# Queries of batch 1: transposed by DMA instead of TensorE, with a new order of all engines and loads

## The chip, the core and the metric

The kernel runs on one core of one Trainium2 chip. The metric is the device time of an execution in microseconds, as the median over runs. One more execution is recorded by the hardware profiler; its page, with all times from the first instruction on, is what is read here.

## The reference

Block-sorted attention for 4 batches of 8 heads (768 positions, 64 wide, 8 blocks of 96), then a Fourier mixing layer and an MLP on the 4 x 768 x 512 result.

```python
P = sort_net                                  # B, H, 8, 8; five Sinkhorn rounds
...
k_sorted = einsum('bhij,bhjcd->bhicd', P, k_blocks)
v_sorted = einsum('bhij,bhjcd->bhicd', P, v_blocks)
scores = scale * matmul(q_block, k_sorted_block^T)
attn = softmax(scores)
x = matmul(attn, v_sorted_block)              # then heads side by side: B, S, 512
mixed = real(fft(fft(x, axis=1), axis=2))
u = x + mixed
un = (u - mean) / sqrt(var + 1e-6)
out = u + maximum(un @ w_ch1, 0) @ w_ch2      # 512 -> 2048 -> 512
```

## The kernel before

The program is a list of operations, each with the engines that can do it, a cost, the tiles that it reads and writes and a priority. A planner (class Plan) runs through a model of the five engines in Python when the kernel is built, gives each operation an engine and a place, and the instructions are then written out in that fixed order. On the chip each engine follows its own list and waits only for semaphores. NUDGE is a table of corrections to the priorities; a smaller priority goes first. An operation on the way to the first MLP is marked as critical and gets a priority of -1000 less the time that still lies behind it; loads are excepted from that.

Of a load the planner knows the bytes. All loads share one modelled stream of Plan.HBM = 390 GB/s (counted in the f32 bytes that are read) and land 2.2 us after it. A DMA transpose, in contrast, is SP time of 1.4 us with a latency of 6.0 us, and carries no bytes:

```python
P.add({"SP": (1.4, 6.0)}, lambda _: nc.sync.dma_start_transpose(...), ..., tag="qX")
```

Loads from HBM are issued by POOL (the helper at L707), and cast f32 to f16 on the way. v of batches 0 and 1 and of batches 2 and 3 come as two tensors of two halves each; k and q come by batch and half (four heads); w1sb in four quarters, w2sb in four quarters. The large loads are all started within the first 40 us or so.

For each batch, attn does four head pairs. kqt (from L1150 on) mixes the blocks of k on TensorE (L1168), evicts it to a tile ks, and makes q's transpose qt. For batches 0 and 1 that is twelve TensorE transposes per pair of heads (L1199), tag qT, and one copy of 128 x 768 out of PSUM by ACT or DVE (L908, tag qtev). For batches 2 and 3, named in QB, load_qk fetches q by single heads, each partition getting a run of 64 elements from each of six places, and one dma_start_transpose on SP's queue (L1186) writes qt. scores (L1227) multiplies, ACT takes the exponent (L1236), L1251 or L1249 subtract one, and av (L1266) multiplies with the mixed v.

Then follow, per batch, the Fourier stages dft1 (L1340 to L1350) and dft2 (L1419, L1431, L1435), which reads the tile rb. The rows of rb are filled by four small copies by SP (a_rows, L1147). After the normalisation, batch 0 is transposed by TensorE (L1528), batches 1 to 3 by DMA (L1520), and the MLP begins: ff1 (L1549) reads w1sb, the second layer (L1606) w2sb. Batches 2 and 3 use a scheme with seven products instead of eight (L1685, L1785).

k and q of batch 1 do not lie in the tile kq but in parts of hr[1], a buffer of the MLP that is still free then (slots 8 to 11).

Of the kernel before, what the change touches and what calls it, by code (L numbers as in the profile page):

```python
# [35 lines left out]
    ('arow', -40.0, 0): 2.49, ('atd', 14.0): -43.53, ('atd', 14.0, 1): 216.41,  # L36
    ('atd', 14.0, 3): -279.13, ('atp', -40.0, 1): 7.79,
# [3 lines left out]
    ('bdk', -90.0, 0): -3.64, ('bdk', -60.0): -1.48, ('bdk', -60.0, 0): 5.16,  # L41
# [3 lines left out]
    ('bna', 20.5): -162.22, ('bna', 40.0): -493.32, ('dft1', 55.0): -1408.65,  # L45
# [8 lines left out]
    ('exp', -80.0, 0): 0.99, ('exp', -80.0, 2): 0.94,  # L54
    ('exp', -80.0, 11): 1.17, ('exp', 10.0): -1038.47,
    ('exp', 10.0, 0): 316.12, ('exp', 10.0, 1): 250.78,
    ('exp', 10.0, 10): -26.46, ('exp', 10.0, 12): 149.24,
    ('exp', 30.0, 0): -340.47, ('exp', 30.0, 4): 130.12,
    ('exp', 30.0, 8): 11.8, ('exp', 30.0, 11): 384.99,
    ('exp', 50.0): -1497.06, ('exp', 50.0, 9): 139.28,  # L60
    ('exp', 50.0, 12): 417.05, ('exp', 50.0, 15): -7.62,
    ('fadd', -300.0): -6.77, ('fadd', -300.0, 4): 378.93,
    ('fadd', -300.0, 10): 1031.06, ('fadd', -300.0, 18): -27.7,
    ('fadd', -300.0, 39): -74.85, ('fadd', -300.0, 40): -359.8,
# [63 lines left out]
    ('ksev', -80.0, 2): -2.56, ('ksev', 10.0): -153.67,  # L128
    ('ksev', 30.0, 4): -239.73, ('ksev', 30.0, 6): -81.13,
    ('ksev', 30.0, 7): -224.44, ('ln', -29.0): -227.5,  # L130
    ('ln', 20.0, 2): -195.03, ('lt', -29.5): -1.65, ('lt', 20.5): 837.52,
    ('lt', 55.5, 1): 117.13, ('mbdk', 50.0): 960.77,
    ('mbdk', 50.0, 0): 242.27, ('norm', -80.0): -10.2,
    ('norm', 10.0, 1): 14.84, ('norm', 10.0, 3): 23.14, ('norm', 30.0): -14.8,
    ('norm', 30.0, 4): 740.67, ('norm', 50.0, 3): -167.68,
    ('oo', 20.0, 0): -370.96, ('pc', -301.0, 16): -181.95,
    ('pk', -70.0, 1): 1.89, ('pmc', -30.0, 0): -4.19, ('pmc', 55.0): -63.31,
    ('pmt', 20.4): 1160.32, ('pmt', 40.0, 0): -47.38, ('pmt', 40.0, 1): -7.96,
    ('pmt', 40.4, 0): -304.8, ('pmt', 55.0, 0): -11.08,
    ('pmt', 55.0, 1): -9.84, ('pmt', 55.0, 2): 529.66,  # L140
    ('pmt', 55.0, 3): 67.16, ('pmt', 55.4, 0): -7.4, ('psa', -40.0): 1.4,
    ('psm', -75.0, 2): 1.23, ('psr', -40.0, 0): 3.56, ('psx', -40.0): 4.36,
    ('qT', 10.0): 67.2, ('qT', 10.0, 0): 32.15, ('qT', 10.0, 1): -345.76,
    ('qT', 10.0, 2): 175.76, ('qtev', -80.0, 0): -0.21,
    ('qtev', 10.0, 3): 148.76, ('relu', -300.0): -61.87,
    ('relu', -300.0, 77): 74.06, ('relu', -300.0, 83): 190.34,
    ('relu', -300.0, 117): 300.59, ('relu', -300.0, 119): 729.75,
    ('relu', -300.0, 125): 206.25, ('res', -300.0): -25.11,
    ('res', -300.0, 11): 93.78, ('res', -300.0, 26): -219.21,
    ('res', -300.0, 28): 40.94, ('res', -300.0, 33): -6.82,  # L150
# [25 lines left out]
QB = (2, 3)  # L176
# [407 lines left out]
def kernel(  # L584
# [84 lines left out]
    rv = ct("rv", [64, DM], F16)  # L669
# [1334 lines left out]
```

## Time and profile before

| | us |
|---|---|
| median of 3 runs | 259.36 (259.25 to 259.37) |
| profiled execution, its time | 258.93 |
| profiled execution, its span | 257.2 |
| PE busy | 247.5 (96%) |
| DVE busy | 240.9 (94%) |
| ACT busy | 159.5 (62%) |
| POOL busy | 54.0 (21%) |

The span goes from the first to the last instruction; what lies around it makes up the difference to the execution's own time. Matmuls are pipelined and their ends are modelled, so that neighbouring groups of PE overlap in a list of instructions; the distance from start to start is the time that a group holds the engine. Of 26.45 MB that the DMA engines wrote, 18.31 MB went through POOL's queue, and almost all of that in the first 70 us.

### The profile page before, as it was taken

Reading aid. Unit: us, or ns where it says so; the run is one execution under the profiler, and the core shown is the slowest. Engines: PE = TensorE matmul, PEld = TensorE weight load, DVE = VectorE, ACT = ScalarE, POOL = GpSimd, SP = SyncE. Lnnn points to the kernel's source line nnn. Section 1 sums busy time; section 2 is a strip of 40 time slices with the busy share of each in tenths; the row PEclk is TensorE's granted clock in tenths of the full one; section 3 lists DMA queues with packets and bytes.
Section 4 is the critical chain, followed back from the end, with each engine's and each line's share of the span. In section 5 each row is a group of like instructions: output and inputs, shape, how many; then the busy total and the mean of one; then the engine's idle time right before and its main releaser. Section 6 shows DMA issues by size and latency. Waiting matters only on the chain.

```text
span 257.2 us, 6684 instructions
## 1 busy us (share of the span) xinstructions
PE 247.5 (96%) x2612; PEld 167.7 (65%) x2612; DVE 240.9 (94%) x608; ACT 159.5 (62%) x360; POOL 54.0 (21%) x81
## 2 busy tenths in 40 slices
PE   4899998999999999999999999999999999999993
PEld 1346875566755576644666657888656888567882
DVE  4799999999999999996999999999999999889993
ACT  2599897899775969918778489100988202685010
POOL 8965222324000390003100000030100011100041
PEclk9999999999999999999999999999999999999999
DMA  7999999999950499533103031221202312200015
GB/s 131 203 219 304 211 217 216 208 210 184 151 41 3 86 179 172 64 62 113 43 18 65 10 66 24 53 101 54 82 3 43 80 71 95 84 1 0 3 69 177
DMA packets 42678, 26.45 MB, mean 103 GB/s; under 512 B 30122, under 2 KB 39096, under 8 KB 42644
## 3 DMA queue, kind: packets, MB, share of 16 engines
q0 software_dynamic: 23536, 18.31, 41.9%
q1 hardware_dynamic: 19110, 7.71, 15.0%
q8 instruction: 20, 0.33, 0.5%
q14 instruction: 12, 0.10, 0.1%
HBM read 29.03 MB, written 6.29 MB: 137 GB/s over the span
## 4 chain that ended last, share of the span: by engine, by line
PE 87%; DVE 8%; DMA 3%; issue 1%; ACT 0%; DVEq 0%; POOLq 0%
PE bank L1785 21%; PE bank L1549 17%; PE bank L1685 14%; PE bank L1606 9%; PE bank L1266 4%; DMA hr<-in_v_dram 3%; PE bank L1431 3%; PE bank L1227 2%; PE bank L1340 2%; PE bank L1168 2%; PE bank L998 2%; PE bank L926 2%; DVE rt L1283 1%; PE bank L1435 1%; PE bank L1971 1%; DVE pmt L1300 1%
## 5 line engine op out<-in xcount | busy, mean ns | idle before, releaser
L1549 PE MATMUL bank<-ut,w1sb 128*128 128x384 f16 x256 | 47.1, 326 | 0.0
L1549 PEld LDWEIGHTS <-w1sb 128*128 128x128 f16 x256 | 23.3, 98 | 14.4
L1584 POOL DMA_INDIRECT out_dram<-u,rows x9 | 9.9, 1105 | 108.3 <-DVE u L1802 74.7
L1785 PEld LDWEIGHTS <-hr 128*128 128x128 f16 x288 | 28.2, 98 | 4.3
L1236 ACT ACTIVATE ex<-bank 96x384 f32<-96x384 f32 x64 | 27.9, 489 | 2.3 <-PE bank L1227 2.0
L1705 ACT COPY vsf<-bank 128x384 f32<-128x384 f32 x48 | 21.6, 484 | 11.0 <-PE bank L1685 10.4
L1561 ACT ACTIVATE hr<-bank 128x384 f16<-128x384 f32 x48 | 23.4, 492 | 8.0 <-PE bank L1549 7.7
L1693 DVE TENSOR_TENSOR hr<-bank,vsf 128x384 f16<-128x384 f32 x48 | 25.1, 553 | 1.4 <-PE bank L1685 0.7
L1816 ACT COPY ex<-bank 128x256 f32<-128x256 f32 x9 | 3.4, 373 | 36.4 <-PE bank L1785 36.3
L1606 PE MATMUL bank<-w2sb,hr 128*128 128x512 f16 x96 | 23.8, 380 | 0.0
L1785 PEld LDWEIGHTS <-vcx 128*128 128x128 f16 x216 | 21.1, 98 | 2.7
L1685 PE MATMUL bank<-ut,w1sb 128*128 128x384 f16 x96 | 20.7, 326 | 0.0
L1785 PE MATMUL bank<-w2sb,hr 128*128 128x256 f16 x144 | 18.5, 272 | 0.0
L1785 PE MATMUL bank<-kq,vcx 128*128 128x256 f16 x144 | 17.8, 273 | 0.0
L1685 PEld LDWEIGHTS <-w1sb 128*128 128x128 f16 x128 | 12.5, 98 | 7.7
L707 POOL DMA_DIRECT2D kq<-in_q_dram x18 | 14.9, 845 | 12.5 <-DMA w2sb<-in_moe_w_ch_dram 3.3
L1283 DVE TENSOR_TENSOR rt<-bank,rz 128x384 f16<-128x384 f32 x32 | 16.9, 545 | 0.1
L1251 ACT ACTIVATE eb<-ex,negone 96x384 f16<-96x384 f32 x28 | 16.8, 620 | 0.2
L1266 PEld LDWEIGHTS <-eb 97*128 97x128 f16 x416 | 15.2, 98 | 2.2 <-issue 0.3
L1266 PE MATMUL bank<-vsf,eb 97*128 97x65 f16 x416 | 16.4, 193 | 0.0
L1249 DVE TENSOR_SCALAR eb<-ex 96x384 f16<-96x384 f32 x36 | 12.5, 366 | 2.3 <-ACT ex L1236 2.3
L908 ACT CAST vsf<-bank 96x512 f16<-96x512 f32 x22 | 13.4, 683 | 1.9 <-PE bank L998 1.9
(190 smaller groups left out, 548.8 us busy)
## 6 DMA issues: line engine op xcount, KB each, us to landing
kq<-in_k_dram POOLq DMA_DIRECT2D x6, 384.0 KB, 7.9
w1sb<-in_moe_w_ch_dram POOLq DMA_DIRECT2D x4, 512.0 KB, 20.2
w2sb<-in_moe_w_ch_dram POOLq DMA_DIRECT2D x4, 512.0 KB, 21.8
hr<-in_v_dram POOLq DMA_DIRECT2D x2, 768.0 KB, 9.1
kq<-in_v_dram POOLq DMA_DIRECT2D x2, 768.0 KB, 16.2
kq<-in_q_dram POOLq DMA_DIRECT2D x16, 96.0 KB, 7.8
out_dram<-u SPq DMA_DIRECT2D x5, 256.0 KB, 2.1
kq<-in_q_dram POOLq DMA_DIRECT2D x2, 384.0 KB, 13.1
```

What stands on the lines that cost most here:

```text
L707: o = P.add({eng: c}, lambda _: e.dma_start(dst, src), r=r, w=w, prio=prio, nbytes=nbytes, tag="load", after=after)
L1236: nc.scalar.activation(ex.ap[0:96], pss[h2].ap[0:96, 0:384], AF.Exp, scale=SCALE),
L1251: nc.scalar.activation(ed, src, AF.Identity, bias=negone[0:96])
L1266: nc.tensor.matmul(po.ap[:, 65 * T:65 * T + 65], eb.ap[:, e0:e0 + 128], vsf[0:97, vi:vi + 65], start=(n == 0), stop=(n == len(WIN[T]) - 1) ...
L1283: P.add({"DVE": (0.465, 0.56)}, lambda _: V.tensor_tensor(rt.ap[:, :, D * h:D * h + D], po3()[:, :, 0:D], rz.ap[:, :, None].broadcast_to([ ...
L1549: nc.tensor.matmul(ps.ap[:, 0:GT], w1sb[:, c, 128 * fc:128 * fc + 128], ut.ap[:, c, :], start=(c == 0), stop=(c == 3))
L1561: nc.scalar.activation(hr[g][:, fc, :], ps.ap[:, 0:GT], AF.Relu)
L1606: nc.tensor.matmul(ps.ap, hr[g][:, fc, 128 * tt:128 * tt + 128], w2sb[:, fc, :], start=(fc == 0), stop=(fc == 15))
L1685: nc.tensor.matmul(ps.ap[:, 0:GT], lhs[:, c, fi], rhs()[:, c, :], start=(start and c == 0), stop=(c == 1), skip_group_check=True)
L1693: return P.add({"DVE": (0.47, 0.57)}, lambda _: V.tensor_tensor(hr[g][:, fc, :], p.ap[:, 0:GT], o.ap, op=ALU.add), r=r, w=hk(g, fc, fc + 1 ...
L1705: P.add({"ACT": act(GT)}, lambda _: nc.scalar.copy(x.ap, A.ap[:, 0:GT]), r=[A], w=[x], prio=pr_v - 1, tag="pc", after=avs)
L1785: nc.tensor.matmul(ps.ap[:, o:o + 256], lhs()[:, fc], rhs[:, fc], start=(start and fc == 0), stop=(fc == 7), skip_group_check=True)
```

## The change

The constant QB takes batch 1 in. With that, q of batch 1 is loaded by single heads (eight loads of 96 KB in place of two of 384 KB), its four pairs are transposed by DMA from SP's queue, and the 48 TensorE transposes and four copies out of PSUM are no longer there. A function slab gives the place of a slot in kq or in hr[1], which the DMA transpose and the load now need. The table NUDGE is a new one: none of its entries has the value that it had, and loads are in it for the first time.

```diff
 NUDGE = {
-    ('arow', -40.0, 0): 2.49, ('atd', 14.0): -43.53, ('atd', 14.0, 1): 216.41,
...
+    ('atd', 14.0): -258.81, ('atd', 14.0, 2): -106.46,
...
+    ('ff1', 100.0): -564.84,
...
+    ('load', -996.0, 0): -3084.429, ('load', -995.0, 0): -2492.353,
+    ('load', -993.0, 0): 1023.837, ('load', 30.0, 0): -3409.518,
+    ('load', 30.5, 0): -3302.183, ('load', 30.52, 0): -3814.411,
+    ('load', 31.0, 0): -0.289, ('load', 31.51, 0): 1.041,
+    ('load', 41.0, 0): -10.289, ('load', 62.0, 0): -31.289,
...
 }
-QB = (2, 3)
+QB = (1, 2, 3)
...
     def qk16(nm, b, hf):
-        n = slot[nm, b, hf]
-        s_ = (kq[:, n, :] if n < 8 else hr[1].rearrange("p a b -> p (a b)")[
-            :, 1536 * (n - 8):1536 * (n - 7)])
-        return s_.rearrange(
+        return slab(slot[nm, b, hf]).rearrange(
             "p (h r d) -> p h r d", h=4, r=6)
+
+    def slab(n):
+        return kq[:, n, :] if n < 8 else hr[1].rearrange(
+            "p a b -> p (a b)")[:, 1536 * (n - 8):1536 * (n - 7)]
...
         if nm == "q" and b in QB:
             for h in range(4):
-                load(kq[:, slot[nm, b, hf], :].rearrange(
+                load(slab(slot[nm, b, hf]).rearrange(
                     "p (a r h d) -> p a h r d", a=2, h=2, d=D)[
                     :, h // 2, h % 2],
                     src[b, 4 * hf + h].rearrange("(r p) d -> p r d", r=6),
-                    260000, [("kq", slot[nm, b, hf], h)], prio + 0.01 * h,
+                    260000, kqk(slot[nm, b, hf], h, h + 1), prio + 0.01 * h,
                     after=after)
...
             P.add({"SP": (1.4, 6.0)}, lambda _: nc.sync.dma_start_transpose(
                 qt.ap.rearrange("p (r s) -> p r s", r=6),
-                kq[:, slot["q", b, hf], 768 * hl:768 * hl + 768]),
+                slab(slot["q", b, hf])[:, 768 * hl:768 * hl + 768]),
                 r=kqk(slot["q", b, hf], 2 * hl, 2 * hl + 2), w=[qt],
                 tag="qX")
```

A key of NUDGE is a tag with the priority as written in the code and, as a third part, the number of the operation among those of that tag and priority. Without nudge, the loads have -994 and -993 for dtab and lt, 19 and 20 for cs and tab, 30 to 31.53 for k and q of batch 1, 31.6 and 31.8 for v of batches 2 and 3, 40 to 43 for w1sb and 62 on for w2sb and what follows.

More of the change, by code (lines that the diff above doesn't have):

```diff
@@ L35 @@
 NUDGE = {
-    ('arow', -40.0, 0): 2.49, ('atd', 14.0): -43.53, ('atd', 14.0, 1): 216.41,
-    ('atd', 14.0, 3): -279.13, ('atp', -40.0, 1): 7.79,
[3 rows of a table removed]
-    ('bdk', -90.0, 0): -3.64, ('bdk', -60.0): -1.48, ('bdk', -60.0, 0): 5.16,
[3 rows of a table removed]
-    ('bna', 20.5): -162.22, ('bna', 40.0): -493.32, ('dft1', 55.0): -1408.65,
[8 rows of a table removed]
[L54 to L64, printed above, removed]
[63 rows of a table removed]
-    ('ksev', -80.0, 2): -2.56, ('ksev', 10.0): -153.67,
-    ('ksev', 30.0, 4): -239.73, ('ksev', 30.0, 6): -81.13,
@@ L130 @@
[L130 to L150, printed above, removed]
[10 rows of a table removed]
-    ('vcd', 70.0): 509.62, ('vcd', 70.0, 2): -49.12, ('vcd', 70.0, 3): -26.03,
-    ('vcd', 70.0, 7): 344.21, ('vcp', -75.0, 1): 2.91,
-    ('vcp', -75.0, 3): 3.09, ('vcp', -75.0, 7): 10.46, ('vev', -50.0): 0.6,
@@ L164 @@
-    ('vev', -50.0, 5): 0.91, ('vev', -50.0, 7): 0.93, ('vev', 9.0, 5): 7.64,
-    ('vev', 12.0, 6): -90.32, ('vev', 12.0, 12): -11.78,
-    ('vev', 12.0, 15): -68.85, ('vmean', -55.0, 2): -1.47,
-    ('vmix', -50.0): -2.39, ('vmix', -50.0, 0): 0.84,
-    ('vmix', -50.0, 7): -7.23, ('vmix', 9.0, 5): 39.01,
-    ('vmix', 12.0): -1403.54, ('vmix', 12.0, 3): -19.6,
-    ('vmix', 12.0, 4): 74.1, ('vmix', 12.0, 5): -23.55,
-    ('vmix', 12.0, 7): -236.78, ('vmix', 12.0, 13): -29.22,
-    ('ws', 90.0, 1): 182.05, ('ws', 90.0, 2): 285.89, ('y', 40.0, 2): -109.37,
+    ('atd', 14.0): -258.81, ('atd', 14.0, 2): -106.46,
@@ new lines @@
+    ('atp', -40.0, 1): 10.64, ('atp', 14.0): 192.74, ('av', -80.0, 3): -0.69,
+    ('av', 10.0): -1020.96, ('av', 10.0, 1): 145.43, ('av', 30.0): -703.12,
+    ('av', 30.0, 3): 1022.43, ('av', 50.0): -271.95, ('bdk', -90.0): 2.31,
+    ('bdk', -60.0): 2.32, ('bdv', -60.0, 0): 1.06, ('bn', 20.0): -257.31,
+    ('bn', 40.0, 2): -198.53, ('bn', 40.5): 87.88, ('bn', 40.5, 0): 211.14,
+    ('bn', 40.5, 2): -175.08, ('bna', 20.0): -208.52, ('dft1', 40.0): -257.71,
+    ('dft1', 40.0, 1): 805.24, ('dft1', 55.0): -410.85,
@@ new lines @@
+    ('dft2', -30.0, 1): 6.25, ('dft2', -29.0, 2): -371.61,
+    ('dft2', 20.0, 2): 88.48, ('dft2', 20.5): 222.15,
+    ('dft2', 20.5, 1): -2.92, ('dft2', 20.5, 2): -2.37,
+    ('dft2', 40.5): -444.69, ('dft2', 55.0, 0): -78.1,
+    ('dft2', 55.0, 1): -23.72, ('dft2', 55.5): -201.24,
+    ('dft2', 55.5, 1): 350.58, ('dft2', 55.5, 2): 513.62,
+    ('em1', 10.0): 249.9, ('em1', 10.0, 15): -281.94, ('em1', 30.0): 325.88,
+    ('em1', 30.0, 14): -19.21, ('exp', -80.0): -4, ('exp', -80.0, 3): -1.32,
@@ new lines @@
+    ('exp', -80.0, 4): -1.72, ('exp', -80.0, 5): -5.33,
+    ('exp', -80.0, 11): -0.74, ('exp', 10.0): -524.78,
+    ('exp', 10.0, 10): 297.83, ('exp', 10.0, 12): -11.68,
+    ('exp', 10.0, 13): -17.87, ('exp', 30.0): 14.21, ('exp', 30.0, 7): 312.64,
+    ('exp', 30.0, 12): -408.4, ('exp', 30.0, 13): -37.31,
+    ('exp', 50.0, 9): 803.77, ('exp', 50.0, 14): 23.79,
+    ('exp', 50.0, 15): 262.41, ('fadd', -300.0): 121.94,
+    ('fadd', -300.0, 13): 179.2, ('fadd', -300.0, 14): -22.27,
[66 rows of a table added]
+    ('kq', 50.0, 2): -39.64, ('ksev', -80.0): 12.78, ('ksev', -80.0, 0): 3.11,
@@ new lines @@
+    ('ksev', 10.0): 98.18, ('ksev', 10.0, 1): -153.31,
+    ('ksev', 10.0, 4): -329.02, ('ksev', 10.0, 7): -266.01,
+    ('ln', -29.0, 2): 253.32, ('ln', 40.0): 42.11,
+    ('load', -996.0, 0): -3084.429, ('load', -995.0, 0): -2492.353,
[3 more added lines that the diff above has]
+    ('load', 41.0, 0): -10.289, ('load', 62.0, 0): -31.289,
+    ('load', 62.0, 1): -25.027, ('load', 62.5, 0): -31.789,
@@ new lines @@
+    ('load', 62.51, 0): -31.799, ('load', 62.52, 0): -31.683,
+    ('load', 62.53, 0): -29.952, ('load', 63.52, 0): -31.063,
+    ('load', 63.53, 0): -30.952, ('load', 64.0, 1): -33.163,
+    ('load', 64.5, 0): -33.663, ('load', 64.52, 0): -33.683,
+    ('load', 64.53, 0): -27.409, ('load', 65.52, 0): -29.431,
+    ('load', 65.53, 0): -34.691, ('lt', -29.5, 0): -1.55, ('lt', 20.0): 229.5,
+    ('lt', 20.0, 0): 170.22, ('mbdk', 30.0, 0): 234.38,
+    ('norm', -80.0, 0): -1.11, ('norm', 10.0, 2): 150.59,
@@ new lines @@
+    ('norm', 30.0, 4): 150.99, ('oo', 20.0, 0): 330.31,
+    ('pmt', -30.0, 0): 1.08, ('pmt', -29.6): 0.88, ('pmt', 20.0, 3): 1.12,
+    ('pmt', 40.0): 374.8, ('pmt', 40.0, 0): -378.76, ('pmt', 55.0, 2): 306.58,
+    ('pmt', 55.4, 0): -368.8, ('psr', 14.0, 0): -312, ('psx', 14.0): -87.92,
+    ('qT', -80.0): 4.2, ('relu', -300.0, 13): 441.92,
+    ('relu', -300.0, 64): 815.83, ('relu', -300.0, 91): 106.88,
+    ('relu', -300.0, 97): 288.27, ('res', -300.0): -574.79,
+    ('res', -300.0, 16): -16.14, ('res', -300.0, 31): 272.2,
[16 rows of a table added]
@@ new lines @@
+    ('vcd', 70.0, 0): -1605.11, ('vcd', 70.0, 2): -14.3,
+    ('vcd', 70.0, 3): -46.89, ('vcd', 70.0, 7): 520.99, ('vcp', -75.0): 7.61,
+    ('vcp', -75.0, 3): 0.42, ('vcp', -75.0, 4): -1.3,
+    ('vcp', -75.0, 6): -1.63, ('vcp', -75.0, 7): 10.14, ('vev', -50.0): 8.11,
+    ('vev', 9.0, 6): 853.35, ('vev', 12.0, 0): 42.91, ('vmean', -55.0): 6.25,
+    ('vmix', -50.0, 1): 0.61, ('vmix', -50.0, 2): 0.65,
+    ('vmix', -50.0, 3): 5.66, ('vmix', -50.0, 4): 3.78,
+    ('vmix', -50.0, 5): 0.76, ('vmix', -50.0, 6): 2.22,
@@ L173 @@
+    ('vmix', 9.0, 2): 1178, ('vmix', 9.0, 5): 300.92,
+    ('vmix', 9.0, 7): 2065.05, ('vmix', 12.0): -833.82,
+    ('vmix', 12.0, 1): -348.45, ('vmix', 12.0, 3): 11.85,
+    ('vmix', 12.0, 7): -654.64, ('vmix', 12.0, 8): -18.63,
+    ('vmix', 12.0, 15): -0.52, ('ws', 90.0): -149.02, ('ws', 90.0, 0): 3.05,
+    ('ws', 90.0, 5): 1348.25, ('y', 20.0, 0): 399.46, ('yz', -29.0): 302.55,
+    ('yz', -29.0, 0): 370.71,
 }
```

169 rows, old and new, of the table NUDGE are left out of this document.

## The prediction

> **What bounds the kernel now.** I read the stages first: busy time of each engine before the first data, up to the first MLP matmul, in the long remainder, and at the end.
>
> ```profile
> 0.00:9.00 9.00, 4.51 (x13) 1.78 (x14) 4.86 (x24) 2.30 (x5) 7.93 (x14) 1.00 0.80 153
> 9.00:51.40 42.40, 41.26 (x614) 26.28 (x613) 40.89 (x114) 37.62 (x76) 18.86 (x28) 1.00 1.16 227
> 51.40:253.20 201.80, 201.69 (x1990) 139.64 (x1986) 194.80 (x473) 119.59 (x280) 27.18 (x40) 1.00 0.44 73
> 253.20:257.20 4.00, 0.00 (x0) 0.00 (x0) 0.36 (x1) 0.00 (x0) 0.00 (x0) 0.92 0.51 171
> ```
>
> The columns after the length are PE, weight loads, DVE, ACT, POOL, granted clock, DMA share and GB/s. From 51.40 on PE is busy for 201.69 of 201.80 us at full clock: whatever PE does not have to do there, and every wait put into it, comes through one to one. The page's chain of what ended last says the same.
>
> ```profile
> PE 87%; DVE 8%; DMA 3%; issue 1%; ACT 0%; DVEq 0%; POOLq 0%
> ```
>
> The stage before it differs: PE, DVE (40.89 of 42.4) and the DMA engines (share 1.16, 227 GB/s) are all full together. The third matters here, because the change swaps PE work for DMA work in that stage. The transposes of batch 1 stand on PE at these places (timeline of PE):
>
> ```profile
> 33.81 0.53 PE L1199 MATMUL bank<-pack,hr 128*64 128x128 f16 x12
> 34.27 0.82 PE L1266 MATMUL bank<-vsf,eb 97*128 97x65 f16 x21
> ...
> 38.29 0.53 PE L1199 MATMUL bank<-pack,hr 128*64 128x128 f16 x12
> 39.35 0.49 PE L1340 MATMUL bank<-cs,eo 128*1 128x386 f16 x2 [0.54 <-DVE eo L1316]
> ...
> 42.44 0.53 PE L1199 MATMUL bank<-pack,hr 128*64 128x128 f16 x12
> 43.07 0.36 PE L1168 MATMUL bank<-bdk,hr 128*64 128x128 f16 x6
> ...
> 43.81 0.38 PE L1435 MATMUL bank<-rb,vcx 97*128 97x512 f16 x1
> ...
> 51.40 0.82 PE L1549 MATMUL bank<-ut,w1sb 128*128 128x384 f16 x4
> ...
> 52.34 0.50 PE L1199 MATMUL bank<-pack,hr 128*64 128x128 f16 x12
> 52.68 0.33 PE L1168 MATMUL bank<-bdk,hr 128*64 128x128 f16 x6
> ```
>
> **Removed: 48 transposes and four evictions.** Going by starts, the group at 33.81 holds PE for 0.46 us and the one at 52.34 for 0.34. The one at 38.29 gives nothing: its successor waits for DVE until 39.35 anyway. The one at 42.44 gives at least the bare 0.34; the further 0.29 to 43.07 is a wait that may stay. Sum 0.46 + 0 + 0.34 + 0.34 = 1.1 us. The ends: 0.34, if only the group behind the first MLP matmul counts, and 4 x 0.53 = 2.1, if the freed time is filled everywhere. I take 1.1, the sum of the steps that the rows show. The evictions:
>
> ```profile
> 36.05 0.78 ACT L908 COPY qt<-bank 128x768 f16<-128x768 f16 x1
> 42.94 1.50 ACT L908 COPY qt<-bank 128x768 f16<-128x768 f16 x2
> 53.48 0.95 DVE L908 COPY qt<-bank 128x768 f16<-128x768 f16 x1
> ```
>
> ACT has idle time in both long stages, so 2.3 us less there costs and brings nothing by itself. DVE's 0.95 us falls behind 51.40, where DVE has 7 us of idle time in 201.8 and PE none; I take 0, with a gain of 0.95 as the other end. It cannot lose.
>
> **Moved: the loads of q.** Two loads of 384 KB become eight of 96 KB with runs of 64 elements. Batches 2 and 3 already use that form. The issues and the rates:
>
> ```profile
> L707 POOL DMA_DIRECT2D kq<-in_q_dram x18 | 14.9, 845 | 12.5 <-DMA w2sb<-in_moe_w_ch_dram 3.3 <-PE bank L1549 2.7 <-DMA w1sb<-in_moe_w_ch_dram 1.7
> 25.00:30.00 5.00, 5.00 (x111) 4.09 (x109) 4.78 (x13) 4.19 (x11) 1.58 (x3) 1.00 1.31 203
> 61.50:63.00 1.50, 1.50 (x16) 0.79 (x15) 1.50 (x5) 1.50 (x4) 0.40 (x2) 1.00 2.35 156
> 69.00:70.50 1.50, 1.50 (x12) 0.90 (x10) 1.50 (x6) 1.38 (x5) 0.00 (x0) 1.00 1.44 117
> 105.00:106.30 1.30, 1.30 (x22) 0.94 (x20) 1.30 (x3) 1.30 (x4) 0.00 (x0) 1.00 0.82 164
> ```
>
> POOL spends 8 x 0.845 - 2 x 0.845 = 5.1 us more on issues. It is busy for 18.86 of 42.4 us and its next loads wait for earlier landings, so I put that at nothing; were that cover gone, the loads would come up to 5.1 us late. In the stretch 25 to 30 the k and q loads of batch 1 run, at 203 GB/s of bytes written; in 61.5 to 63 the small loads run, at 156. Eight times 98,304 B at 156 is 5.0 us, two times 393,216 B at 203 is 3.9: 1.2 us more on the DMA engines.
>
> **Added: four DMA transposes,** each of a 128 x 768 tile of f16, 196,608 B. Behind 69 they run beside the tail of the loads (117 GB/s), from 105 alone (164 GB/s): 1.7 and 1.2 us each. None of today's eight stands in the loaded stage; they are issued from 64 on. Landing takes 4.3 to 8.9 us, and SP is held 1.22 us by an issue:
>
> ```profile
> L1186 SPq DMA_TRANSPOSE qt<-kq x8: 1212/1219/2288, 64.1 to 118.6; - x8
> DMA to landing us min/median/max: 4.3/5.8/8.9
> ```
>
> The Trainium skill ("Advanced Engine Details and Errata", X-Bar Transpose (TRN2)) states that transposing DMAs are as fast as regular ones, with an expected 350-400 GB/s. By it one takes an estimated 0.56 us at 350 GB/s; the two stretches above moved 117 and 164 GB/s, so this trace does not agree.
>
> What is late next is the first MLP weight. Its last quarter is the fourth of these loads:
>
> ```profile
> 28.73 0.53 POOL L707 DMA_DIRECT2D w1sb<-in_moe_w_ch_dram x1 [1.41 <-DMA hr<-in_q_dram]
> w1sb<-in_moe_w_ch_dram POOLq DMA_DIRECT2D x1, 512.0 KB, 21.1
> ```
>
> It lands at 28.73 + 21.1 = 49.8, after 21 us in a queue that never runs dry, and the fourth matmul of the group at 51.40 reads it at about 51.40 + 0.5 = 51.9. That is 2.1 us of lead. The new load priorities in the diff pull one quarter of w1 ahead of v's second half (41.0 - 10.289 = 30.711, against 31.6), but leave the other three at 40, 42 and 43, behind v and behind every q load of batch 1. The planner knows the bytes of loads: at its 390 GB/s the eight cost 0.51 MB or 1.3 us more, and it orders PE around that. A transpose it takes for SP time and a latency of 6.0 us, without bytes. So the unplanned delay of w1 is 3 to 4 transposes (the last may run beside w1 itself) at 1.2 to 1.7 us, 3.6 to 6.8 us. I take 3.5 at 1.2 = 4.2, the lower price because the engine share of 2.35 shows that small packets overlap. Less the lead of 2.1, PE stands still for 2.1 us at its first w1 group; the ends are 1.5 and 4.7. PE's order is fixed, so nothing behind that group can move forward, and no stage behind it has slack to repay it.
>
> **Sum.** The profiled execution took 258.93 us (span 257.2, 1.7 outside it), 0.4 below the median of 259.36. 258.93 - 1.1 + 2.1 = 259.9, and with the 0.4 to the median 260.4 us: slower by 1.0. A difference of 0.2%, 0.5 us, is about what a measurement of this kernel can tell from no change.
>
> The rest of the diff is the new table of priorities. It changes no instruction's duration. The trace shows almost no wait of PE behind 45 us that a better order could remove, so I give it no gain of its own; bounds by the rows are -0.8 us (the waits of 0.54 at 39.35 and 0.29 at 43.07) and as much again above.
>
> **Rivals.**
>
> *Faster: w1 is in time.* If the new order starts w1's first group some 2 us later and has scores and values of batch 1 to do meanwhile, the stall is gone and PE's relief stays: -1.1 to -2.1, around 257.8 us. For it: PE was full between 45 and 51.4 with such work, ACT has 2.3 us more for it, and the q loads of the first half now go out before dtab and the tables. Against: w1's first group got a priority of 100 - 564.84, so the planner starts it as soon as it believes w1 landed, and PE, DVE and DMA are all full there. The skill's rule on transposes belongs here; as a mechanism of this kernel it is the case that four transposes delay w1 by less than the 2.1 us of lead, under 0.6 us each, half of what the cheapest stretch shows.
>
> *Slower by more: the rows of rb.* The four small copies into rb are on the way to the first MLP:
>
> ```profile
> L1147 SPq DMA_DIRECT2D rb<-rr x3: 587/627/631, 34.0 to 36.0; - x3
> rb<-rr SPq DMA_DIRECT2D x1, 32.0 KB, 6.4
> ```
>
> The last is issued at 36.0, lands at 42.4 and is read at 43.81: 1.4 us of lead. They share SP's queue with the new transposes. One transpose that is unfinished in front of them costs 1.2 us of issue and 1.2 to 1.7 of transfer; from one on, the lead is used up, and two cost PE some 4 us. Half of that may be covered by w1's being late anyway, so 2 us more, 262.4. For it: the loads of q's first half end before 30. Against: the planner treats these copies as urgent and the first two transposes have 4 us before them.
>
> *Gain and stall cancel:* if the transposes in front of w1 delay it by some 3.2 us in all (fewer than three at 1.2), the stall of 3.2 - 2.1 equals the 1.1 saved, and the time stays within 0.5 us of 259.36. That the change doesn't do what it says can be left out: the branch in kqt is taken by the batch number.
>
> **How the numbers follow.** Forecast (w1 late, 259.9 to 262) 0.42; faster 0.40; cancelled 0.08; rows of rb late as well 0.10. So faster 0.40, same 0.08, slower 0.52. Likeliest time 260.4. For the range, the faster case ends at 259.36 - 2.1 = 257.3, and the slower one, with the stall at 4.7 and 1.1 saved, at 263.0; these take in most of both.
>
> **What would show it.** Right: PE's first group on w1sb has idle time in front of its last quarter's matmul, put down to the landing of w1sb, of 1.5 to 4.7 us, with w1's last quarter landing at 54 or later; the transposes of batch 1 move some 120 to 160 GB/s and take 6 us or more to land; PE has 48 instructions less; the stage behind the first MLP matmul is as full as now and as long, less about 0.3. Wrong: if w1 lands before PE asks for it, or PE has other work until then, the forecast fails at that step and the time falls to 258; if the rows of rb come after 44 us, the last rival holds.

## The result: slower by 5.6%, and where the time went

| | before | after |
|---|---|---|
| median, us | 259.31 (4 runs) | 273.78 (273.45 to 274.2, 4 runs) |
| ratio to before | | 1.0563 (95% interval 1.0543 to 1.0583) |
| profiled execution: time, span | 258.93, 257.2 | 274.0, 272.2 |

The stages of after, in the columns shown before the change (length, PE, weight loads, DVE, ACT, POOL, granted clock, DMA share, GB/s):

```profile
0.00:9.00 9.00, 4.83 (x12) 1.75 (x13) 4.87 (x24) 2.31 (x5) 6.08 (x12) 1.00 0.79 144
9.00:51.40 42.40, 35.72 (x543) 22.70 (x542) 38.99 (x93) 32.16 (x64) 24.20 (x33) 0.96 1.33 211
51.40:100.00 48.60, 42.56 (x477) 26.43 (x476) 40.04 (x91) 32.78 (x76) 8.83 (x11) 0.93 1.01 120
100.00:150.00 50.00, 49.83 (x586) 29.92 (x585) 45.75 (x102) 39.89 (x93) 9.13 (x14) 1.00 0.62 85
150.00:200.00 50.00, 50.00 (x426) 36.51 (x425) 49.23 (x125) 27.00 (x64) 4.65 (x6) 1.00 0.24 57
```

From 100 on PE is as full as it was. The whole loss lies ahead of that: PE has 6.7 us of idle time in the stage from 9 to 51.4 (1.1 before) and 6.0 in the next. The list of what PE waited for (total, times, longest) names two new waits, and in the page's chain the share of DMA goes from 3% to 7%:

```profile
PE bank L1238 <- DMA qt<-hr: 6.0, 1, 6.0
PE bank L889 <- DVE hr L879: 4.4, 1, 4.4
PE bank L1982 <- DMA pack<-k_pack: 3.8, 1, 3.8
...
PE 80%; DVE 8%; DMA 7%; ACT 2%; issue 1%; DVEq 0%
```

The third was there before (3.7). The landmarks on PE's timeline, with the idle time in brackets:

```profile
18.11 0.27 PE L889 MATMUL bank<-hr,pack 64*128 64x256 f16 x1 [4.38 <-DVE hr L879]
...
47.83 0.49 PE L1351 MATMUL bank<-cs,eo 128*1 128x386 f16 x2
...
57.41 0.50 PE L1238 MATMUL bank<-qt,ks 64*128 64x96 f16 x8 [5.97 <-DMA qt<-hr]
...
68.94 1.31 PE L1560 MATMUL bank<-ut,w1sb 128*128 128x384 f16 x7
```

The first Fourier matmul came at 39.35 before and comes at 47.83 (8.5 later), the first w1 group at 51.40 before and at 68.94 (17.5 later). From there to the end it is 205.8 us before and 203.3 after: 2.5 us are won back, and 17.5 - 2.5 = 15.0 is the difference of the spans.

**Wait A: POOL's memsets.** The nudges on loads pull five loads of k and q ahead of POOL's memsets. POOL then waits for a landing of v as well, and the memset of eb runs at 11.04 instead of 4.78. First two lines of POOL and one of DVE in before, then the same in after:

```profile
4.78 6.16 POOL L777 MEMSET eb<- 96x1672 f16 x4
10.82 0.16 POOL L789 MEMSET negone<- 128x1 f32 x1
...
11.49 0.79 DVE L908 COPY vcx<-hr 128x768 f16<-128x768 f16 x1
```

```profile
9.48 0.83 POOL L717 DMA_DIRECT2D hr<-in_q_dram  x1 [2.34 <-DMA hr<-in_v_dram]
...
11.04 6.13 POOL L788 MEMSET eb<- 96x1672 f16 x4
...
11.48 6.25 DVE L919 COPY vcx<-hr 128x768 f16<-128x768 f16 x1
17.66 0.40 DVE L879 TENSOR_TENSOR hr<-bank,pack 64x256 f16<-64x256 f32 x1
```

The same copy by DVE takes 6.25 us beside the memset, 0.79 without it, and ends at 17.73, as POOL's last memset ends (17.77). The Sinkhorn step behind it (L879) is what PE waits for at 18.11. The short f32 operations of DVE at the same time keep their 0.2 us. The Trainium skill ("SBUF — State Buffer", Who interferes with whom) says that DVE and GpSimd share a pair of ports, that copy is among the operations that can take it, and that whoever issues first holds it for the whole instruction. The memset began first and the copy took 6.25 us, which agrees; here the copy was held up through four memsets, not one.

**Wait B: the transposes take turns with the loads.** SP's queue, then the chain, then the DMA issues of 30 to 70 us (last number: median us from issue to landing):

```profile
30.52 1.32 SPq L1197 DMA_TRANSPOSE qt<-hr  x1
37.75 1.93 SPq L1158 DMA_DIRECT2D rb<-rr  x3
...
40.48 16.29 SPq L1197 DMA_TRANSPOSE qt<-hr  x3
...
40.48 16.89 DMA qt<-hr
...
qt<-hr SPq DMA_TRANSPOSE x4, 15.0
```

Of the four landings two are on record, the first transpose's after 14.8 us and the last one's after 15.1; the chain gives the second 16.89 us, some 5 of them behind the first, which landed at 45.3. A transpose moves 196,608 B, but as 768 packets of 256 B. What the two queues moved in 35 to 40 us, and then in 55 to 60 us (packets, MB, and the time that the packets took as a share of the 16 engines' time; q0 is POOL's queue of loads, q1 SP's):

```profile
q0 software_dynamic: 178, 1.00, 96.2%
q1 hardware_dynamic: 179, 0.05, 6.8%
...
q0 software_dynamic: 785, 0.78, 92.2%
q1 hardware_dynamic: 786, 0.19, 29.9%
```

In both stretches the two queues get the same number of packets through, whatever their size. While the loads come in packets of some 5,600 B (1.00 MB / 178), SP's queue gets 179 packets through in 5 us; at 994 B per load packet it gets 786. At the lower rate 768 packets take an estimated 21 us, at the higher one 4.9, and up to three transposes are queued. The transposes' own packets are short: 6.8% of 16 x 5 us for 179 is an estimated 30 ns each, against an estimated 430 ns for a load packet (96.2% for 178). All 768 would keep 16 engines busy for an estimated 1.5 us; the rest of the time to land is waiting. The Trainium skill ("DMA: Bandwidth & Descriptors", Queues, rings and completion order) states that each DMA engine goes round its queue rows packet by packet; 178 to 179 and 785 to 786 agree.

**The clock behind the waits.** In two stretches of after the granted clock is half; these are the windows in them and right behind them:

```profile
18.60:22.00 3.40, 3.40 (x25) 1.45 (x24) 3.40 (x9) 0.56 (x2) 2.92 (x5) 0.50 1.37 200
22.00:25.00 3.00, 2.99 (x46) 1.64 (x45) 2.09 (x7) 2.98 (x7) 1.38 (x3) 1.00 1.29 378
...
57.41:62.90 5.49, 5.49 (x26) 3.01 (x27) 2.54 (x10) 2.82 (x7) 1.64 (x2) 0.50 1.22 196
63.00:66.00 3.00, 3.00 (x28) 1.46 (x27) 2.40 (x8) 2.49 (x9) 0.75 (x1) 1.00 1.21 195
```

The granted clock is 0.50 for the first 3.4 us or so behind wait A and for the first 5.5 us behind wait B. Busy time by the half that is missing gives an estimated 3.40 x 0.50 = 1.7 us and 5.49 x 0.50 = 2.7 us. So from 39.35's counterpart to the first w1 group the 9.1 us more are 6.0 of wait and 2.7 of clock, which leaves 0.4; ahead of it the 8.5 us are 4.4 of wait and 1.7 of clock, and 2.4 are spread over later landings and PE waits that I did not trace one by one.

### The profile page after: what moved, and what is told of

The parts are those of the page before. It is cut to its first block, busy times and chain, and to the rows that moved or that the text cites. A ratio compares the mean times of both kernels' runs of the same rounds, so it can differ in the third digit from the quotient of the medians.

```text
span 272.2 us, 6582 instructions
## 1 busy us (share of the span) xinstructions
PE 250.3 (92%) x2563; PEld 168.5 (62%) x2563; DVE 244.1 (90%) x602; ACT 162.4 (60%) x362; POOL 62.1 (23%) x87
## 4 chain that ended last, share of the span: by engine, by line
PE 80%; DVE 8%; DMA 7%; ACT 2%; issue 1%; DVEq 0%
PE bank L1796 20%; PE bank L1560 15%; PE bank L1696 13%; PE bank L1617 8%; DMA qt<-hr 6%; PE bank L1277 4%; PE bank L1442 3%; PE bank L1238 2%; DVE vcx L919 2%; PE bank L1179 2%; PE bank L1009 2%; PE bank L1351 2%; PE bank L937 2%; PE bank L1446 2%; PE bank L1111 1%
## 5 line engine op out<-in xcount | busy, mean ns | idle before, releaser
L1247 ACT ACTIVATE ex<-bank 96x384 f32<-96x384 f32 x64 | 27.9, 484 | 10.1 <-PE bank L1238 9.5
L1560 PEld LDWEIGHTS <-w1sb 128*128 128x128 f16 x256 | 23.3, 98 | 14.5 <-issue 0.2
L1716 ACT COPY vsf<-bank 128x384 f32<-128x384 f32 x48 | 22.1, 482 | 10.6 <-PE bank L1696 10.1
L1796 PEld LDWEIGHTS <-vcx 128*128 128x128 f16 x216 | 21.1, 98 | 2.9
L717 POOL DMA_DIRECT2D kq<-in_q_dram x18 | 14.8, 835 | 18.6 <-PE bank L1356 6.6
L919 ACT CAST ks<-bank 128x384 f16<-128x384 f32 x25 | 11.2, 481 | 12.4 <-PE bank L1179 12.3
L1238 PE MATMUL bank<-qt,ks 64*128 64x96 f16 x256 | 10.6, 207 | 7.0 <-DMA qt<-hr 6.0
```

The lines of the kernel that those rows point to most:

```text
L919: (nc.scalar.copy if e == "ACT" else V.tensor_copy)(dst, src)
L1247: nc.scalar.activation(ex.ap[0:96], pss[h2].ap[0:96, 0:384], AF.Exp, scale=SCALE),
L1560: nc.tensor.matmul(ps.ap[:, 0:GT], w1sb[:, c, 128 * fc:128 * fc + 128], ut.ap[:, c, :], start=(c == 0), stop=(c == 3))
L1716: P.add({"ACT": act(GT)}, lambda _: nc.scalar.copy(x.ap, A.ap[:, 0:GT]), r=[A], w=[x], prio=pr_v - 1, tag="pc", after=avs)
L1796: nc.tensor.matmul(ps.ap[:, o:o + 256], lhs()[:, fc], rhs[:, fc], start=(start and fc == 0), stop=(fc == 7), skip_group_check=True)
```

## The experiments

Theory T: the loss is A (memsets beside DVE's copy) plus B (transposes slowed by turns with load packets). Rivals: the new order itself costs, or the swap costs wherever it stands. Medians in us; the ratio is to before on the same chip. The new order with TensorE transposes was not run.

| run | what it is | time | ratio (95%) |
|---|---|---|---|
| e1_memsets_first | after, memsets early | 270.1 | 1.0404 (1.0376 to 1.0433) |
| e2_small_packets | after, smaller load packets | 269.85 | 1.039 (1.0355 to 1.0424) |
| e3_both | e1 and e2 | 266.72 | 1.0266 (1.0228 to 1.0303) |
| e4_plain_copy | after, copies for transposes | 265.07 | 1.0221 (1.0197 to 1.0246) |
| e8_memsets_plain | e1 and e4 | 259.58 | 0.9999 (0.9981 to 1.0017) |
| e12_memsets_plain_look | the same kernel as e8, one run | 259.06 | none |
| e7_before_memsets_late | before, memsets late | 265.83 | 1.0235 (1.0214 to 1.0256) |
| e6_old_order_packets | before's table, e2's packets | 267.82 | 1.0326 (1.0267 to 1.0385) |
| e5_old_order | before's table | 278.8 to 286.94 | none, the runs differ too much |
| e11_old_order_again | the same kernel as e5 | 287.39 | 1.109 (1.1035 to 1.1145) |
| e9_q_early | e3, one q load earlier | 262.4 | 1.0115 (1.0091 to 1.0138) |
| e10_replanned | e3's edits, table searched anew | 265.65 | 1.0249 (1.0217 to 1.028) |

### Each cause alone

The memsets are put back ahead of POOL's fifth load; no other engine's list changes:

```diff
-        for o in P.schedule():
+        plan = P.schedule()
+        early = [o for o in plan if o.eng == "POOL" and o.tag in (
+            "ebz", "ksz", "vsz", "small")]
+        plan = [o for o in plan if o not in early]
+        at_ = [n for n, o in enumerate(plan) if o.eng == "POOL"][4]
+        plan[at_:at_] = early
+        for o in plan:
```

> The changed kernel, with one edit: POOL's memsets stand ahead of its fifth load again, as before the change; nothing else in the order is touched. Theory T (two separate causes: memsets on POOL that overlap a copy on DVE hold up the chain of the Sinkhorn result, and q's transposes land late because their packets take turns one for one with the packets of the loads): DVE's copy of 128 x 768 takes 0.8 us in place of 6.25, PE's wait of 4.4 us at 18.1 is gone, but the second transpose still lands at about 55.5, because the stream of loads sets that and not the moment of issue; so the time falls by 1.5 to 3 us only, to 271 to 272. Rival R1 (the wait at 18 us goes through to the end, the transposes only add what they cost in bytes): about 5 to 6 us less, 268.

270.1 us, 3.7 less: more than T's 1.5 to 3, less than the 5 to 6 of R1. The copy takes 0.80 us and the wait at L889 is gone (that matmul starts at 13.32), but PE, now earlier, waits longer for qt, until 47.27 and again until 63.32; the landing at 55.5 that T gave does not show:

```profile
PE bank L1238 <- DMA qt<-hr: 9.4, 2, 7.4
PE bank L1988 <- DMA pack<-k_pack: 3.7, 1, 3.7
```

Next the load packets. w1sb is fetched in quarters of columns, so that a run is 1024 B, and v's second tensor in runs of 768 B. The keys that ff1 waits for stay the same.

```diff
-        load(w1sb[:, c, :], w1v[:, c, :], 1048576, [("w1", c)], prio)
+        load(w1sb[:, :, 512 * c:512 * c + 512],
+             w1v[:, :, 512 * c:512 * c + 512], 1048576, [("w1", c)], prio)
...
+        if t == 1:
+            load(nat[1].rearrange("p (j t x) -> p t j x", t=2, x=384)[
+                :, hf], ...)
```

> The changed kernel, with the loads of w1 and of the second v cut so that a packet holds 1024 and 768 bytes in place of 4096 and 6144; the same bytes in the same number of loads, and the order of all engines as it is. T (turns by packet): a transpose lands within 8 to 10 us of issue in place of 15 to 17, PE's wait of 6.0 us for qt at 57.4 falls under 1 us, and its clock stays at 1.0 in 55 to 65; the wait at 18 us stays. About 266. Rival R2 (the transposes are late because the DMA engines have too many bytes to move, so that packets do not matter): same waits, 273 to 276.

269.85 us: not the 266 expected, but below R2's 273. The same bytes in smaller load packets bring the first and the last transpose from 14.8 and 15.1 us to 10.1 and 10.8, a little over T's 8 to 10. The wait for qt falls to 3.5 us and not under 1, and the granted clock is 0.81 in 60 to 65, where T had 1.0:

```profile
PE bank L896 <- DVE hr L886: 4.4, 1, 4.4
PE bank L1989 <- DMA pack<-k_pack: 3.7, 1, 3.7
PE bank L1245 <- DMA qt<-hr: 3.5, 2, 2.6
```

Both edits together (e3):

> Both edits, memsets first and small packets. T: neither wait is left, 258 to 262; the two gains are not a sum, because the early one only shows when the late one is gone. R1: the sum of the two single gains.

266.72 us, above the 258 to 262 expected, and close to R1's sum of the two gains (3.7 + 3.9 less is 266.2). One wait of 4.5 us for qt is left: the last transpose is issued at 48.76, when the last head of q, queued behind v, has landed at 48.6, and takes 9.9 us more.

### The transposes replaced by copies of the same bytes

```diff
-            P.add({"SP": (1.4, 6.0)}, lambda _: nc.sync.dma_start_transpose(
+            P.add({"SP": (1.4, 6.0)}, lambda _: nc.sync.dma_start(
+                qt.ap, slab(slot["q", b, hf])[:, 768 * hl:768 * hl + 768])
+                if b == 1 else nc.sync.dma_start_transpose(
```

> The changed kernel, with batch 1's four DMA transposes replaced by plain copies of the same 196,608 bytes on the same queue in the same place (q is then not transposed for batch 1, so that part of the computation is left out). A copy has 128 packets of 1536 bytes where a transpose has 768 of 256. T (turns by packet): eight turns for each engine in place of 48, landing 5 to 9 us after issue, no wait for qt, about 266. R2 (bytes): landing and time as in the changed kernel, 273 to 275.

265.07 us, about as T had it. The copies have 128 packets of 1536 B instead of 768 of 256, and the two landings on record came after 7.2 and 9.8 us; the wait for qt is gone, the 4.4 us at L889 stays. The bytes, the queue and the places in SP's list are those of after, and the first two are issued at 30.67 and 40.54 (30.52 and 40.48 in after). Two things differ, though: the number of packets, and that nothing is transposed; an issue also holds SP for 0.6 us at most, where it was up to 10.25. This run alone doesn't tell them apart. The packet rows of after do: a transpose's packets took an estimated 30 ns each in both stretches shown (77 in 40 to 45, 68.7% for 715), against 430 for a load's at the time of the long wait, so the transposing itself was not what was slow, and e2, which does transpose, gains from smaller load packets. The copies take turns just as well: in 45 to 50 the two queues of this run got 228 and 230 packets through.

With the memsets early as well:

> The changed kernel with the memsets first and plain copies in place of batch 1's DMA transposes (q of batch 1 is then not transposed, so that part of the computation is left out). T: nothing is left of the loss but what the new loads themselves cost: 257 to 260. Rival (the new order has a third fault): 261 or more, with a wait of PE that names it.

259.58 us, ratio 0.9999: with both causes gone, the loss is gone, and the new order shows no third fault. The four kernels make a square:

| | memsets late | memsets early |
|---|---|---|
| transposes | 273.78 | 270.1 |
| copies | 265.07 | 259.58 |

A is worth 5.5 us where nothing else is late and 3.7 where qt waits anyway; B is worth 8.7 or 10.5. Together 14.2 of the 14.5 us. The same kernel was looked at once more for its profile (259.06 us):

> The kernel of e8_memsets_plain once more for its profile (q of batch 1 is copied, not transposed, so this part of the computation is left out). Theory T: no wait of PE over 1 us between 5 and 80 us, clock 1.00 in every stretch, memsets done by 11.5, the copies land in 7 to 10 us, first w1 group at 53.5 to 55; 259 to 260. Rival: a wait for qt of 1 to 2 us that eats the planned gain.

```profile
53.97 1.47 PE L1562 MATMUL bank<-ut,w1sb 128*128 128x384 f16 x8
...
PE bank L1990 <- DMA pack<-k_pack: 3.7, 1, 3.7
PE bank L937 <- DMA hr<-in_v_dram: 1.0, 1, 1.0
PE bank L1179 <- DVE un L919: 0.8, 1, 0.8
PE bank L1279 <- DVE rt L1296: 0.3, 1, 0.3
```

No wait for qt, clock 0.999. In this profile PE is busy for 246.2 us, 1.3 less than before's 247.5, and idle for 11.1 instead of 9.7; but the first profile of the same kernel (260.76 us) has 248.5 us busy. So the two do not show PE's relief, and the time doesn't either.

A in the other direction, on before, with the memsets put behind its ninth operation of POOL:

> The kernel before the change, with one edit: POOL's memsets stand behind its ninth load, where the changed kernel has them. T: one copy on DVE takes about 6 us in place of 0.8, PE waits 4.4 us for it at about 17 us and its clock drops behind it; 4.4 to 6.5 us more, 264 to 265.5. Rival: the wait at 18 us comes from something else in the new order: 259 to 260.

265.83 us, 6.5 more and 0.3 above T's range, without any DMA transpose of batch 1 in it:

```profile
10.70 6.17 POOL L777 MEMSET eb<- 96x1672 f16 x4
...
11.60 5.82 DVE L908 COPY vcx<-hr 128x768 f16<-128x768 f16 x1
...
PE bank L1023 <- DVE hr L868: 4.2, 1, 4.2
```

A needs neither the swap nor the new table, only the place of the memsets.

### The old order with the swap in it

After's code with before's table of priorities, less its entry of tag psx. First, with e2's packets ("the run before it" in the text on record is e5, below):

```diff
 NUDGE = {
...     # before's entries
 }
 QB = (1, 2, 3)
```

> The same with the small packets of w1 and of the second v. T: a transpose lands 5 us or more earlier than in the run before it, and half or more of the loss goes: 261 to 265. R2 and R3: no gain, or 1 us more for the slower loads.

267.82 us, 2.8 above the upper end, and 19.6 below the same order with after's packets (e11, below). Apart from the 3.8 us at the start, the longest of its waits is a new one:

```profile
PE bank L1443 <- DMA rb<-rr: 3.3, 1, 3.3
...
27.94 8.31 SPq L1194 DMA_TRANSPOSE qt<-hr  x3
36.36 1.25 SPq L1155 DMA_DIRECT2D rb<-rr  x2
```

Three transposes stand on SP's queue ahead of the rows of rb. These are issued from 36.36 on (34.0 in before), and the matmul that reads them starts at 47.93 after 3.3 us of idle time (43.81 in before). With after's packets:

> The DMA transposes of batch 1 without the new order: the changed kernel with the table of priorities of the kernel before, less its two entries for the operation psx (with them the planner finds no order), so that memsets and loads are in their old places and q of batch 1 goes out in eight loads. The planner expects 0.7 us more than for the kernel before. T (turns by packet): the rows of rb and the later transposes stand behind transposes that take turns with packets of v and w1; PE waits 5 to 12 us in the stretch 42 to 62, 266 to 272. R2 (bytes alone, as predicted): 260 to 262. R3 (the new order, not the transposes, made the loss): 259 to 260.

> The kernel of e5_old_order once more, since its runs lay between 278.8 and 286.9: after's code with before's table of priorities, packets as in after. Theory T (turns packet by packet): the transposes are issued about 28 and take 14 to 17 us each way beside packets of 4096 and 6144 B, rows of rb stand behind them on SP's queue and land 50 or later, so PE waits for rb 8 to 12 us ahead of the first w1 group: 272 to 280. Rival (the new table is what costs, the swap itself is cheap): 260 to 262. Rival D (the chip was disturbed): under 270.

The first time the runs lay between 278.8 and 286.94 us and give no ratio; the second time they took 286.52 to 290.12, 287.39 in the median, so rival D falls. Both profiles show the same two waits (14.1 and 9.9 us in e5). The time is beyond every expectation, T's 272 to 280 too; here is e11:

```profile
PE bank L1436 <- DMA rb<-rr: 14.4, 1, 14.4
PE bank L999 <- issue: 10.4, 1, 10.4
...
28.08 27.80 SPq L1187 DMA_TRANSPOSE qt<-hr  x3
55.99 1.25 SPq L1148 DMA_DIRECT2D rb<-rr  x2
...
L1187 SPq DMA_TRANSPOSE qt<-hr x4: 1222/2022/21112, 28.1 to 80.0; - x4
```

One issue holds SP for 21.1 us, so the rows of rb are issued at 55.99 instead of 34.0. So the rival "the new table is what costs" falls: on the same swap the new table is worth 287.39 - 273.78 = 13.6 us. It puts the rows of rb between the transposes, and after has no wait for them; how much of the 13.6 us is due to that is not shown, as the 10.4 us at L999 are not explained. Nor is it shown what holds SP. In 35 to 40 the DMA engines moved 40 GB/s and were busy for a share of 0.55 (212 GB/s in after in the same stretch); what held them, the records don't show, and e6 with its smaller packets moved 191 GB/s there.

### Can an order hide it?

e3 with the late head of q loaded ahead of v's second tensor:

```diff
+        late = [o for o in plan if o.tag == "load" and o.prio0 == 31.51][0]
+        plan.remove(late)
+        plan.insert([n for n, o in enumerate(plan) if o.tag == "load"
+                     and o.prio0 == 31.6][0], late)
```

> e3_both with one more step of POOL's order: the last single head of q of batch 1's second half is loaded ahead of v's second tensor instead of behind it. In e3_both that head landed at 48.6, the last two transposes were issued at 48.76 and landed at 58.67, and PE stood still 4.5 us for qt. Theory T (what remains in e3_both is the wait for the last transposes, whose source came late and which then took 9.9 us beside w1 and w2): the head lands before 40, the last transposes land by 52, the wait for qt falls from 4.5 us to under 1.5, first w1 group at 55 to 57, time 260 to 263. Rival K (the transposes are simply too slow beside any load, wherever they stand: moved earlier, they wait for one another, and v comes later): the wait for qt stays above 3 us or turns into a wait for v or w1, time 265 to 267.

262.4 us, in T's range, and 3.1 above before. The last transpose still takes 13.6 us (issued at 40.69, landed at an estimated 54.3, where T had 52), but PE doesn't wait for it any more. Waits for loads take its place:

```profile
PE bank L944 <- DMA hr<-in_v_dram: 1.6, 1, 1.6
PE bank L944 <- DMA kq<-in_v_dram: 1.5, 1, 1.5
PE bank L1567 <- DMA w1sb<-in_moe_w_ch_dram: 1.2, 1, 1.2
```

Last, the planner told the truth as measured in e2, and its table searched anew:

```diff
-            P.add({"SP": (1.4, 6.0)}, ...
+            P.add({"SP": (1.4, 10.5 if b == 1 else 6.0)}, ...
...
+        for o in P.ops:
+            if o.tag in ("ebz", "ksz", "vsz", "small") and "POOL" in o.costs:
+                o.prio = -4996.5
```

> after, with three things told to its planner: batch 1's transposes take 10.5 us to land (not 6.0), POOL's memsets come ahead of POOL's loads as in before, and w1 and the second tensor of v come in packets of 1024 and 768 B. Then a new table of priorities searched for with that plan. Planned end 254.4; before is planned at 255.7 and took 259.3, so the same surplus would give 258.0. Theory T (the loss came from a plan that priced transposes at 6.0 us and moved the memsets, not from the swap itself): no wait for qt over 1.5 us, memsets done by 11 us, first w1 group at 53 to 56, time 258 to 261. Rival K (transposes beside the loads cost more than any order can hide: SP held, rows of rb behind transposes): waits for qt or rb of 3 us or more in all, time 263 to 267.

265.65 us: T's 258 to 261 fails, the rival's range holds. The first w1 group starts at 54.86, as T had it, but one wait for qt of 3.7 us stands at 64.30. The two last heads of q were put behind v and two quarters of w1 and landed at 48.9 and 49.6; the transposes went out at 49.08 and 50.45. The first landed at 59.1, about as planned (10.0 us); the landing of the other isn't in the records, but PE waited until 64.30, 13.8 us after its issue. One number for the landing doesn't describe an operation whose time depends on what else is queued. No version here beats the kernel before; of those that compute the whole result, e9 comes nearest.

## Why the prediction was wrong

The sign was right, the size was not: 260.4 forecast, 273.78 measured, outside 257.3 to 263.0. Nor does the sign support the mechanism: the loss came through two waits for which the sum had no term, and the stall at w1 that it did have is not there.

- **The price of a transpose**, "at 1.2 to 1.7 us", is the first step that failed. I took the time that its bytes keep the DMA engines busy, from stretches behind 69 us, for all that it delays. As engine time that was about right (an estimated 1.5 us above). But beside loads a transpose gets one packet through for each packet of theirs, and lands after 14.8 to 16.9 us. My own sign for it, "6 us or more to land", had no upper end, and the median of 5.8 us in before's rows came from 64.1 us on, when v and w1 had landed.
- **What is late next** failed with it: not w1, but the transposes' own result. I never asked when PE needs qt. PE stood still for it for 6.0 us at 57.41. I followed the bytes to w1, whose last quarter was to land 4.2 us later than 49.8. It landed at 54.6, which agrees with the forecast by luck: its load was issued at 34.3 instead of 28.73, and took 20.3 us instead of 21.1, so no lengthening by the transposes shows. PE did not ask for w1 until 68.94. Only in e9, with the two other waits gone, does PE stand still for w1 (1.2 us at 57.78, its second group on it).
- **The rest of the diff, costed at nothing** (bounds of 0.8 us) is the second failure: "It changes no instruction's duration." It made DVE's copy 6.25 us long instead of 0.79, and PE waited 4.4 us behind it. I asked what the new table could gain on PE and not what the nudges on loads are moved past. POOL's memsets stand on the same queue as the loads; e7 puts 6.5 us on their place alone.
- **The rows of rb.** The mechanism is real: 3.3 us in e6, 14.4 in e11. In after the new order avoids it: the rows are issued from 37.75, between the transposes, and none of PE's listed waits in after is for rb. The rival had a chance of 0.10 and 2 us; where it strikes it is larger.
- **The relief of PE**, 1.1 forecast, is not shown. The two profiles of e8's kernel have PE busy for 1.3 us less and for 1.0 us more than before, and its time is that of before. So "comes through one to one" is not borne out.
- **The clock** was not in the sum. Behind the two waits it cost an estimated 1.7 and 2.7 us.
- **The rule of the Trainium skill** that transposes run as fast as other transfers, named in the prediction ("Advanced Engine Details and Errata", X-Bar Transpose (TRN2)), does not hold beside these loads: 196,608 B in 15.0 us are 13 GB/s, and e4's copies of the same bytes were faster.

## What to carry to other kernels

Price a transfer that runs beside others by its packets, and by the packets of the queue next to it, not by bytes: where two queues take turns one for one, as here, the queue of small packets loses, and what stands behind it on its issuing engine can wait too. Ask first who waits for the transfer itself. When priorities of loads change, look at everything else on the engine that issues them, and at what that work runs beside in its new place. A planner that gives an operation one fixed latency may move it to where that latency is least true; check the landing in the trace before searching again.

## What the runs showed of the hardware

- Two queues with work got equal numbers of packets through: 178 and 179 beside load packets of some 5,600 B, 785 and 786 beside load packets of 994 B in after, 228 and 230 in e4 with copies in place of transposes.
- A packet of 256 B took an estimated 30 ns in after, and all 768 of a transpose still needed some 15 us to land.
- A DVE copy of 128x768 f16 takes 0.79 us alone, 6.25 beside memsets on POOL in after and 5.82 in e7.
- A single issue on SP held the engine for 10.25 us in after and for 21.1 us in e11, where the prediction reckoned with 1.22.
- Behind PE's waits of 4.4 and 6.0 us in after the granted clock was 0.50 for an estimated 3.4 and 5.5 us of PE's work, then 1.00.
